# Agent attention before two feed-forward layers: scores with agents on partitions, one maximum, all weights decoded ahead of the loop

## The chip, the cores and the metric

One core of one Trainium2 chip runs the whole program. The metric is the device time of one execution in microseconds (us). The kernel before has a median of 1144.72 us over 3 runs (1144.35 to 1146.73).

## What is computed

The reference, cut to what matters (q, k, v are 12480 x 128, there are 49 agents, the hidden size of both layers is 2048):

```python
def _attn_ref(q, k, v, agents):
    scale = 1.0 / np.sqrt(q.shape[-1])
    def sm(a, b):
        s = scale * (a @ b.transpose(0, 2, 1))
        s = s - s.max(-1, keepdims=True)
        e = np.exp(s)
        return e / (e.sum(-1, keepdims=True) + 1e-09)
    agent_v = sm(agents, k) @ v
    return sm(q, agents) @ agent_v

def _moe_ref(x, w_in, w_out):
    h = x @ w_in
    g = np.where(h >= 1, h, np.where(h <= -1, 0.0, (h + 1) ** 2 / 4))
    return g @ w_out

def _moe2_ref(x, w_in, w_out, s, b):
    r = np.maximum(x @ w_in, 0.0)
    return (s * (r * r) + b) @ w_out
```

The output is `_moe2_ref(_moe_ref(_attn_ref(...)))`. The weights arrive as 64-bit floats; the kernel decodes them itself into a high and a low part, both fp32r.

## The kernel before, in words

**The preparation** (`prologue`, `agents_values`, L292 to L528) makes the agents' values and folds them into the first layer's weights. An order written out by hand, the string SEQ (L52), sets how its steps are issued; each engine runs its own instructions in that order. Keys and values come in 14 groups of 7 chunks of 128 tokens. For each group `score` (L372) makes one matmul per chunk, with the keys as the stationary operand, so tokens lie on partitions and agents in columns; ACT copies the scores to SBUF (L378), and `peak` (L387) keeps a running maximum on DVE. Groups 0 to 6 form a first half, groups 7 to 13 a second. For each half the maximum per agent is found (L392), transposed by PE (`turn`, L399), reduced (L403) and spread over all partitions by a matmul (`spread`, L410). Then `power` subtracts it on POOL (L420) and ACT takes the exponential (L423), and `average` (L434) multiplies with the values, even and odd chunks into the two halves of PE's columns. The first half's sums are scaled to the second half's maximum and both are added (L502). The sums are normalised (L504 to L513), and `aw` (L520 to L526) multiplies them with the first layer's input weights in four blocks of 512 columns; two blocks share one PSUM tile.

**Decoding** (`decode`, L230) takes each of the four weight matrices in two pieces of 1024 columns: A0 A1 (first input weights), B0 B1 (first output weights), C0 C1 and D0 D1 (second layer). A piece costs five instructions on DVE (L244, L254, L261, L270, L275) and three on ACT (L245, L248 and the high copy L265), all on 128 x 1024. They are issued in order by the letter w in SEQ (31 of them), and what is left over when the preparation ends is issued in the loop, one at each W of ORDR or ORD, or by need (L699 to L706). Eight small instructions on DVE make each tile of the query softmax (L164 to L177, letter z in SEQ and `fill` in the loop).

**Loads** go through SP's queue in the order of LOADS (L58). `pump` issues a load as soon as SEQ has passed the step that frees its buffer: 10 buffers of keys and values, 3 of weights (1 MB each). POOL sets a column of ones in each tile of values (L333), so a row of sums comes with the averages. The letter d in SEQ is a dummy matmul on zeros (`dummy`, L466).

**The loop** (L691) walks over 25 blocks of tokens (the first has 256 columns, 23 have 512, the last 448) with eight steps each. A step issues on PE H1, O1, H2, O2 (L573, L655), on ACT the ReLU and the square (L589 to L595), on DVE the cap (L599) and the low part (L615), and the high copy by a pattern (L608, L610): in the first twelve steps it is a cast on POOL. The second layer lags by 11 steps. For the first 11 steps the order of a step's other instructions is ORDR:

```python
    NR, ORDR, ORD = 11, (
        "T2 R1 Y y V R2 Q G2 C2 W S1 L1 L2 M1 Z F c1 G1 F"
```

R1 and S1 are the ReLU and the square, L1 the low part of the step before, M1 the cap, c1 the cast, F a step of a query softmax. `column_sums` (L544) adds up the rows of the second output weights in 32 small matmuls, six a step, once their piece is decoded; a small DVE instruction (L550) closes it.

Of the kernel before, what the change touches and what calls it, by code (L numbers as in the profile page):

```python
# [11 lines left out]
I32 = mybir.dt.int32  # L12
# [6 lines left out]
def kernel(  # L19
# [25 lines left out]
    GR, XB, UB, WB, KV = 3, 3, 3, 2, 10  # L45
    WARM, CD = 12, 2
# [4 lines left out]

    SEQ = (  # L52
# [4 lines left out]
    )  # L57
    LOADS = (  # L58
        "k0 A0 k1 k2 A1 k3 k4 B0 k5 k6 B1 k7 k8 q0 v0 k9 v1 k10 v2 k11 C0 v3 k12 v4 k13 v5 v6 q1 v7 v8 v9 v10 "
        "v11 v12 v13 C1 D0 D1"  # L60
# [4 lines left out]
        "T2 R1 Y y V R2 Q G2 C2 W S1 L1 L2 M1 Z F c1 G1 F"  # L65
    ).split(), (
        "R1 T2 S1 V Q Y G2 R2 C2 L1 W F M1 y W L2 F Z G1 c1 W"
    ).split()
    QS, QT, CSN, EA, DX = 3, 1, 6, 3, 1
# [9 lines left out]
    chunks = [(c0, min(P, NT - c0)) for c0 in range(0, NT, P)]  # L79
    NCH = len(chunks)  # L80
    GC = 7
    groups = [list(range(g, min(g + GC, NCH))) for g in range(0, NCH, GC)]
    NG = len(groups)
# [7 lines left out]
    dec = ctx.enter_context(tc.tile_pool(name="dec", bufs=1))  # L91
# [15 lines left out]
    aT2 = const.tile([P, 2 * NA], F32, name="aT2")  # L107
    aT = aT2[:, 0:NA]
# [119 lines left out]
    decoded = [0]  # L228

    def decode(weights):  # L230

        first, last = [], []
        for src, dst_h, dst_l, i in weights:
            sl = slice(i * WC, (i + 1) * WC)
            t = {}

            def exponent(t=t, src=src, i=i):
                u = wu.pop((src.name, i))
                words = u.rearrange("p (n two) -> p n two", two=2)
                t["e"] = u[:, 0:WC]  # L240
                t["lo"], t["hi"] = words[:, :, 0], words[:, :, 1]
                w = dec.tile([P, 2 * WC], U32, tag="t", name="wt", bufs=WB)
                t["y"], t["z"] = w[:, 0:WC], w[:, WC:2 * WC]
                nc.vector.tensor_scalar(out=t["y"], in0=t["hi"], scalar1=MASK_H, scalar2=None, op0=ALU.bitwise_and)  # L244
                acts.append(lambda: nc.scalar.activation(  # L245
                    out=t["z"].bitcast(I32), in_=t["lo"], func=ACTF.Copy, scale=XS
                ))
                acts.append(lambda: nc.scalar.activation(  # L248
                    out=t["y"].bitcast(I32), in_=t["y"], func=ACTF.Relu, scale=8.0, bias=wbias[:, 0:1]
                ))  # L250

            def rest(t=t):
                run_acts()
                nc.vector.scalar_tensor_tensor(  # L254
                    out=t["z"], in0=t["hi"], scalar=23, in1=t["z"], op0=ALU.logical_shift_left, op1=ALU.bitwise_or
                )

            def sign(t=t, sl=sl, dst_h=dst_h):
                run_acts()
                y = t["y"]  # L260
                nc.vector.scalar_tensor_tensor(  # L261
                    out=y, in0=t["hi"], scalar=0x80000000, in1=y, op0=ALU.bitwise_and, op1=ALU.bitwise_or
                )
                acts.append(
                    lambda: nc.scalar.activation(out=dst_h[:, sl], in_=y.bitcast(F32), func=ACTF.Copy)  # L265
                )

            def power(t=t):
                run_acts()
                nc.vector.tensor_scalar(  # L270
                    out=t["e"], in0=t["y"], scalar1=0xFF800000, scalar2=None, op0=ALU.bitwise_and
                )

            def low(t=t, sl=sl, dst_l=dst_l):
                nc.vector.scalar_tensor_tensor(  # L275
                    out=dst_l[:, sl], in0=t["z"], scalar=2.0 ** -43,
                    in1=t["e"].bitcast(F32), op0=ALU.mult, op1=ALU.mult,
                )
                decoded[0] += 1

            first.append(exponent)
            last.append([rest, sign, power, low])
        ops = [first[0]]
        for i, rest in enumerate(last):
            ops += rest[:EA] + first[i + 1:i + 2] + rest[EA:]
        return ops
# [5 lines left out]
    def prologue():  # L292
        with ExitStack() as pctx:
            pro = pctx.enter_context(tc.tile_pool(name="pro", bufs=1))
            wi1h = pro.tile([P, DFF], F32R, name="wi1h")
            wi1l = pro.tile([P, DFF], F32R, name="wi1l")
            agents_values(pro, wi1h, wi1l)

    def agents_values(pro, wi1h, wi1l):
# [4 lines left out]
        half = {"A": range(0, (NG + 1) // 2), "B": range((NG + 1) // 2, NG)}  # L304
        cut = half["B"][0]
        S = pro.tile([P, NCH, LO], F32, name="S")
        mx = pro.tile([P, GC, NA], F32, name="mx")
        diag = pro.tile([P, NA], F32, name="diag")
        fold = pro.tile([P, 1], F32, name="fold")
        rden = pro.tile([P, 1], F32, name="rden")  # L310
        eps = pro.tile([P, 1], F32, name="eps")
        avs = pro.tile([P, C + 1], F32, name="avs")
        avn = pro.tile([P, C], F32, name="avn")
        twice = pro.tile([P, P], F32, name="twice")
        avh = pro.tile([P, P], F32R, name="avh")
        avl = pro.tile([P, P], F32R, name="avl")
        mx1, mt, mcol, mbs, av = {}, {}, {}, {}, {}
# [6 lines left out]
        def keys(g):  # L324
            c0, c1 = chunks[groups[g][0]][0], sum(chunks[groups[g][-1]])
            kv["k", g] = pro.tile([P, GC * (C + 1)], F32, tag="kv", name=f"k{g}", bufs=KV)
            nc.sync.dma_start(out=kv["k", g][:, :c1 - c0], in_=kT[:, c0:c1])

        def values(g):
            full = [c for c in groups[g] if c < NFULL]  # L330
            t = pro.tile([P, GC * (C + 1)], F32, tag="kv", name=f"v{g}", bufs=KV)
            t = kv["v", g] = t.rearrange("p (c d) -> p c d", d=C + 1)
            nc.gpsimd.memset(t[:, :, C:C + 1], 1.0)  # L333
            nc.sync.dma_start(out=t[:, :len(full), :C], in_=v_main[:, full[0]:full[-1] + 1, :])
            if len(full) < len(groups[g]):
# [22 lines left out]
        def parts(g):  # L358

            cs = groups[g]  # L360
            for n in sorted({chunks[c][1] for c in cs}, reverse=True):
                own = [c for c in cs if chunks[c][1] == n]
                yield n, own[0], own[-1] + 1

        def score(g):

            scv = ps_h(f"ks{g}").rearrange("p b (c a) -> p (b c) a", a=P)
            c1 = groups[g][0]
            base = chunks[c1][0]
            for c in groups[g]:  # L370
                c0, n = chunks[c]
# [406 lines left out]
```

## Time and profile before

| | before |
|---|---|
| median of 3 runs | 1144.72 us |
| the profiled execution | 1145.62 us |
| its span, first to last instruction | 1143.8 us |
| PE busy (share of the span) | 1113.0 us (97%) |
| DVE busy | 986.1 us (86%) |
| ACT busy | 961.4 us (84%) |
| POOL busy | 33.8 us (3%) |
| mean granted TensorE clock | 0.981 |

The busy times are sums over the whole execution. PE's matmuls overlap, so that a busy PE is one with a matmul in flight. The granted clock is a share of 2.4 GHz; 0.5 is the lower of its two levels, 1.2 GHz.

### The profile page before, as it was taken

Reading aid. Unit: us, or ns where it says so; the run is one execution under the profiler, and the core shown is the slowest. Engines: PE = TensorE matmul, PEld = TensorE weight load, DVE = VectorE, ACT = ScalarE, POOL = GpSimd, SP = SyncE. Lnnn points to the kernel's source line nnn. Section 1 sums busy time; section 2 is a strip of 40 time slices with the busy share of each in tenths; the row PEclk is TensorE's granted clock in tenths of the full one; section 3 lists DMA queues with packets and bytes.
Section 4 is the critical chain, followed back from the end, with each engine's and each line's share of the span. In section 5 each row is a group of like instructions: output and inputs, shape, how many; then the busy total and the mean of one; then the engine's idle time right before and its main releaser. Section 6 shows DMA issues by size and latency. Waiting matters only on the chain.

```text
span 1143.8 us, 13561 instructions
## 1 busy us (share of the span) xinstructions
PE 1113.0 (97%) x5167; PEld 910.7 (80%) x5167; DVE 986.1 (86%) x1181; ACT 961.4 (84%) x1109; POOL 33.8 (3%) x50
## 2 busy tenths in 40 slices
PE   7878999999999999999999999999999999999998
PEld 6767788888888888888888888888888888888887
DVE  6568798988898898898998898898898898898886
ACT  4446798898988989989989988988989989889886
POOL 1333100000000000000000000000000000000000
PEclk9677999999999999999999999999999999999999
DMA  9930000000000000000000000000000000000000
GB/s 341 315 121 9 1 15 1 19 19 1 19 19 1 19 19 1 19 19 1 19 19 1 19 19 1 19 19 1 19 19 1 19 19 9 10 10 10 1 10 17
DMA packets 27312, 34.86 MB, mean 30 GB/s; under 512 B 1968, under 2 KB 19056, under 8 KB 26736
## 3 DMA queue, kind: packets, MB, share of 16 engines
q1 hardware_dynamic: 27248, 34.00, 9.2%
q8 instruction: 40, 0.66, 0.2%
q14 instruction: 24, 0.20, 0.1%
HBM read 27.61 MB, written 6.39 MB: 30 GB/s over the span
## 4 chain that ended last, share of the span: by engine, by line
PE 89%; DVE 4%; ACT 2%; issue 1%; POOL 0%; POOLq 0%; DVEq 0%; ACTq 0%
PE h L573 39%; PE o L655 24%; PE y L655 23%; PE qs L147 2%; DVE x L599 1%; PE tp L190 1%; PE avA L434 1%; DVE gl L615 1%; PE ks L372 0%; ACT x L595 0%; ACT x L589 0%; DVE wt L254 0%; ACT wt L248 0%; POOL gh L610 0%; PE aw L520 0%
## 5 line engine op out<-in xcount | busy, mean ns | idle before, releaser
L615 DVE TENSOR_TENSOR gl<-x,gh 128x1024 fp32r<-128x1024 f32 (+2 forms) x399 | 476.4, 1194 | 15.1 <-POOL gh L610 6.3
L595 ACT ACTIVATE x<-x 128x1024 f32<-128x1024 f32 (+2 forms) x399 | 392.0, 1032 | 0.6
L589 ACT ACTIVATE x<-h 128x1024 f32<-128x1024 f32 (+2 forms) x200 | 201.6, 1008 | 111.1 <-PE h L573 111.1
L599 DVE SCALAR_TENSOR_TENSOR x<-h,x 128x1024 f32<-128x1024 f32 (+2 forms) x200 | 238.9, 1195 | 57.3 <-ACT x L595 53.4
L591 ACT ACTIVATE x<-h 128x1024 f32<-128x1024 f32 (+2 forms) x199 | 199.4, 1002 | 7.8 <-PE h L573 7.8
L610 DVE CAST gh<-x 128x1024 fp32r<-128x1024 f32 (+1 forms) x243 | 165.3, 681 | 38.5 <-ACT x L595 38.5
L655 PE MATMUL y<-gh,wo1h 128*128 128x512 f32 (+2 forms) x400 | 160.5, 401 | 3.1 <-POOL gh L610 2.1
L655 PE MATMUL y<-gl,wo1h 128*128 128x512 f32 (+2 forms) x400 | 157.8, 394 | 2.8 <-DVE gl L615 2.7
L573 PE MATMUL h<-pt,awh 128*128 128x512 f32 (+2 forms) x400 | 157.7, 395 | 0.8 <-ACT pt L195 0.8
L573 PE MATMUL h<-yh,wi2h 128*128 128x512 f32 (+2 forms) x400 | 156.0, 390 | 1.0 <-ACT x L591 0.8
L655 PE MATMUL y<-gh,wo1l 128*128 128x512 f32 (+2 forms) x400 | 156.7, 392 | 0.0
L573 PE MATMUL h<-pt,awl 128*128 128x512 f32 (+2 forms) x400 | 156.7, 392 | 0.0
L655 PE MATMUL o<-gl,wo2h 128*128 128x512 f32 (+2 forms) x400 | 156.0, 390 | 0.0
L573 PE MATMUL h<-yl,wi2h 128*128 128x512 f32 (+2 forms) x400 | 155.8, 390 | 0.0
L655 PE MATMUL o<-gh,wo2l 128*128 128x512 f32 (+2 forms) x400 | 155.8, 389 | 0.0
L655 PE MATMUL o<-gh,wo2h 128*128 128x512 f32 (+2 forms) x400 | 155.8, 389 | 0.0
L573 PE MATMUL h<-yh,wi2l 128*128 128x512 f32 (+2 forms) x400 | 155.7, 389 | 0.0
L608 ACT ACTIVATE gh<-x 128x1024 fp32r<-128x1024 f32 (+1 forms) x144 | 149.0, 1035 | 1.3 <-DVE x L599 1.2
L655 PEld LDWEIGHTS y<-gl,wo1h 128*128 128x128 f32 x400 | 76.2, 190 | 22.1 <-DVE gl L615 5.4
L655 PEld LDWEIGHTS y<-gh,wo1h 128*128 128x128 f32 x400 | 76.5, 191 | 19.6 <-POOL gh L610 3.5
L573 PEld LDWEIGHTS h<-pt,awh 128*128 128x128 f32 x400 | 76.3, 191 | 17.8 <-ACT pt L195 0.9
L573 PEld LDWEIGHTS h<-yh,wi2h 128*128 128x128 f32 x400 | 75.1, 188 | 19.0 <-ACT x L591 1.2
(124 smaller groups left out, 1040.1 us busy)
## 6 DMA issues: line engine op xcount, KB each, us to landing
q<-in_qT SPq DMA_DIRECT2D x23, 256.0 KB, 2.8
out_T<-osb SPq DMA_DIRECT2D x23, 256.0 KB, 2.0
k<-in_kT SPq DMA_DIRECT2D x13, 448.0 KB, 9.3
v<-in_v_main SPq DMA_DIRECT2D x13, 448.0 KB, 6.4
wu<-in_w_in SPq DMA_DIRECT2D x4, 1024.0 KB, 7.4
wu<-in_w_out SPq DMA_DIRECT2D x4, 1024.0 KB, 8.0
k<-in_kT SPq DMA_DIRECT2D x1, 416.0 KB, 8.4
v<-in_v_main SPq DMA_DIRECT2D x1, 384.0 KB, 4.7
```

The costliest lines, as they stand in the source:

```text
L147: nc.tensor.matmul(out=scv[:, i, :], lhsT=qt[:, c0:c0 + P], rhs=aT, start=True, stop=True)
L190: nc.tensor.matmul(out=tp[:, c0:c0 + P], lhsT=ptok[t % NPT][:, i, :], rhs=ident_r, start=True, stop=True,)
L434: nc.tensor.matmul(out=av[h][r, :], lhsT=S[:n, c, :], rhs=kv["v", g][:n, i, :], start=(c == same[0]), stop=(c == same[-1]),)
L573: nc.tensor.matmul(out=h[:, i, :w], lhsT=a[:, sl], rhs=r, start=(m == 0), stop=(m == len(ops) - 1))
L589: nc.scalar.activation(out=x, in_=h, func=ACTF.Relu, scale=0.5, bias=0.5)
L591: nc.scalar.activation(out=x, in_=h, func=ACTF.Relu)
L595: nc.scalar.activation(out=x, in_=x, func=ACTF.Square)
L599: nc.vector.scalar_tensor_tensor(out=x, in0=h, scalar=1.0, in1=x, op0=ALU.max, op1=ALU.min)
L608: nc.scalar.activation(out=a, in_=x, func=ACTF.Copy)
L610: (nc.gpsimd if kind == "2" else nc.vector).tensor_copy(out=a, in_=x)
L615: nc.vector.tensor_tensor(out=b, in0=x, in1=a.bitcast(F32), op=ALU.subtract)
L655: nc.tensor.matmul(out=o[:, :w], lhsT=l[:, c, :], rhs=r[:, i, :w], start=(c == 0 and m == 0), stop=(c == KF - 1 and m == 2),)
```

## The change

The preparation is rewritten; the loop loses its decoding and keeps everything else.

- **Scores** have agents on partitions: the agents (padded to 64) are the stationary operand, 512 keys the moving one, and a group of 1024 keys fills the two halves of the partitions. There are 13 groups. ACT copies a group (S), DVE reduces it to one column (m).
- **One maximum** for all keys, in place of two halves and their fold: a reduce (r), two tiny matmuls that swap the partition halves (w), and the negative scaled maximum as a column (c). The exponential (E) takes it as its bias, so POOL subtracts nothing.
- **Exponentials are transposed back** by PE, four transposes a group (t), copied from PSUM by DVE for groups 0, 3, 6, 9, 12 and by ACT for the others (V), into three buffers; then the averages (a) as before, all into one sum.
- **Decoding** is named step by step in SEQ (A0.0 is L244's step of piece A0, .1 and .2 ACT's two, .3 to .7 the rest). All eight pieces stand in SEQ. The high copy (.5) goes from ACT to POOL.
- **Agents' weights** use four PSUM tiles, one a block, in the three buffers.
- **Buffers**: 7 for keys and values (of 8 chunks), 4 for weights; the decoder's buffers belong to the preparation.
- SEQ has 43 dummies in place of 13, 38 of them ahead of r; 10 warm-up matmuls in place of 12.

The diff, cut to its core:

```diff
-    GR, XB, UB, WB, KV = 3, 3, 3, 2, 10
-    WARM, CD = 12, 2
+    GR, XB, UB, WB, KV = 3, 3, 4, 2, 7
+    WARM, CD = 10, 2
...
+        "d d d d A0.1 A0.0 d d A0.2 A0.3 d s0 A0.4 s1 S0 m0 A0.5 d S1 A0.6 d m1 d A1.1 A0.7 d d d A1.0 s2 A1.3 "
+        "A1.2 d s3 S2 A1.4 s4 S3 m2 A1.5 m3 d S4 A1.6 d m4 d A1.7 B0.1 d d d B0.0 s5 B0.3 B0.2 d s6 S5 B0.4 s7 S6 "
+        "m5 B0.5 m6 d S7 B0.6 d m7 d B0.7 B1.1 d d d B1.0 s8 B1.3 B1.2 d s9 S8 B1.4 s10 S9 m8 B1.5 B1.6 d S10 m9 d "
+        "m10 d B1.7 C0.1 d d d C0.0 s11 C0.3 C0.2 s12 q0 S11 C0.4 S12 d z0.0 d m11 C0.5 d C1.1 m12 d z0.1 r z0.2 d "
+        "C0.6 w z0.3 z0.4 d c z0.5 d C0.7 E0 d E1 t0 E2 z0.6 C1.3 t1 E3 t2 V1 V0 d t3 V2 z0.7 C1.0 a0 E4 z0.8 E5 "
+        "z0.9 a1 V3 E6 D0.0 E7 a2 E8 a3 E9 E10 t4 E11 t5 V4 t6 V5 t7 V6 a4 E12 C1.2 t8 V7 t9 C1.4 t10 D0.2 C1.6 "
+        "C1.5 D0.1 a5 D0.4 V8 a6 C1.7 D1.1 D0.5 t11 V9 a7 D0.3 t12 V10 a8 D1.3 p0 V11 a9 D0.6 P0 D1.0 q1 V12 D1.2 "
+        "D0.7 a10 z1.0 D1.4 a11 z1.1 a12 D1.5 D1.6 z1.2 z1.3 D1.7 z1.4 z1.5 z1.6 z1.7 z1.8 z1.9"
...
+    VDVE = (0, 3, 6, 9, 12)
...
+        "A0 k0 k1 A1 k2 k3 k4 B0 k5 k6 k7 B1 k8 k9 k10 C0 k11 k12 q0 C1 v0 v1 v2 D0 v3 q1 v4 D1 v5 v6 v7 v8 v9 v10 "
+        "v11 v12"
...
-        "T2 R1 Y y V R2 Q G2 C2 W S1 L1 L2 M1 Z F c1 G1 F"
+        "T2 R1 Y y R2 Q G2 C2 S1 L1 L2 M1 Z F c1 G1 F"
...
+        def high():
+            nc.gpsimd.tensor_copy(out=dst_h[:, sl], in_=t["y"].bitcast(F32))
...
         def score(g):
+            sc[g] = ps_h(f"ks{g}")[:, 0, :]
+            for r, t0, n in halves(g):
+                x = t0 - g * GT
                 nc.tensor.matmul(
+                    out=sc[g][r, :n], lhsT=a64, rhs=kv["k", g][:, x:x + n], start=True, stop=True
                 )
             free["kv"] += 1
...
+        def score_copy(g):
+            for r, c in areas(g):
+                nc.scalar.activation(out=ST[r, c], in_=sc[g][r, :c.stop - c.start], func=ACTF.Copy)
...
         def peak(g):
+            for r, c in areas(g):
+                nc.vector.tensor_reduce(out=mxs[r, g:g + 1], in_=ST[r, c], op=ALU.max, axis=AX.X)
+
+        def peaks():
+            nc.vector.tensor_reduce(out=m1, in_=mxs, op=ALU.max, axis=AX.X)
+
+        def other():
+            sw.append(ps_h("sw")[:, 0, 0:2])
+            for i, x in enumerate((ident, swap)):
+                nc.tensor.matmul(out=sw[0][:, i:i + 1], lhsT=x, rhs=m1, start=True, stop=True)
+
+        def column():
+            nc.vector.tensor_reduce(out=m1, in_=sw[0], op=ALU.max, axis=AX.X)
+            nc.vector.tensor_scalar_mul(nm, m1, -scale)
...
         def power(g):
+            for r, c in areas(g):
+                nc.scalar.activation(
+                    out=ST[r, c], in_=ST[r, c], func=ACTF.Exp, scale=scale, bias=nm[r, 0:1]
                 )
+
+        def turn(g):
+            tp[g] = ps_h(f"st{g}")[:, 0, :]
+            for j in range(4 if g < NG - 1 else 1):
+                sl = slice(g * TB + j * P, g * TB + (j + 1) * P)
+                nc.tensor.transpose(out=tp[g][:, j * P:(j + 1) * P], in_=ST[:, sl], identity=ident)
+
+        def turn_copy(g):
+            n = TB if g < NG - 1 else P
+            tok[g] = pro.tile([P, TB], F32, tag="tok", name=f"tok{g}", bufs=3)
+            if g in VDVE:
+                nc.vector.tensor_copy(out=tok[g][:, :n], in_=tp[g][:, :n])
+            else:
+                nc.scalar.activation(out=tok[g][:, :n], in_=tp[g][:, :n], func=ACTF.Copy)
...
+            for j in range(4 if g < NG - 1 else 1):
+                for h in range(2):
+                    n = REST if h and g == NG - 1 else P
+                    x = j * P + h * LO
+                    nc.tensor.matmul(
+                        out=av[0][h * LO:(h + 1) * LO, :], lhsT=tok[g][:n, x:x + LO],
+                        rhs=kv["v", g][:n, 4 * h + j, :], start=(g == 0 and j == 0), stop=(g == NG - 1),
+                    )
...
-        column_sums(NSUM)
-        nc.vector.tensor_tensor(out=avs, in0=av["B"], in1=avs, op=ALU.add)
+        nc.vector.tensor_copy(out=avs[:, C:C + 1], in_=av[0][:, C:C + 1])
         den = ps_h("den")[:, 0, 0:1]
         nc.tensor.matmul(out=den, lhsT=twice, rhs=avs[:, C:C + 1], start=True, stop=True)
+        nc.vector.tensor_copy(out=avs[:, :C], in_=av[0][:, :C])
...
-        nc.vector.reciprocal(out=rden, in_=den)
+        nc.vector.tensor_scalar_add(rden, den, 1e-9)
+        nc.vector.reciprocal(out=rden, in_=rden)
...
-        for i in range(DFF // (2 * TB)):
-            aw = ps_h(f"aw{i}")
-            for b in range(2):
...
+        for i in range(DFF // TB):
+            aw = ps_h(f"aw{i}")[:, 0, :]
+            sl = slice(i * TB, (i + 1) * TB)
...
-            while wfill and decoded[0] <= max(map(WORD.index, need), default=-1):
-                wfill.pop(0)()
-                feeds[0]()
-                run_acts()
...
-            column_sums(NSUM if n == D + 1 else CSN)
+            column_sums(CSN)
...
-                if c == "V": run_acts()
-                if c == "W":
-                    if wfill:
-                        wfill.pop(0)()
-                        feeds[0]()
```

## Rows read from the trace of the kernel before

**Rows 1.** Stretches: length; busy us of PE, PEld, DVE, ACT, POOL; clock; DMA share; GB/s.

```profile
0.00:35.00 35.00, 27.23 (x164) 24.14 (x165) 23.88 (x40) 16.49 (x22) 3.10 (x14) 0.91 0.99 347
...
35.00:60.00 25.00, 20.23 (x153) 17.73 (x151) 14.04 (x24) 9.87 (x19) 9.11 (x17) 0.70 1.03 305
...
60.00:76.60 16.60, 13.79 (x123) 11.51 (x122) 13.44 (x22) 9.41 (x18) 8.83 (x8) 0.71 0.45 146
...
85.00:112.00 27.00, 22.05 (x112) 19.62 (x111) 21.88 (x34) 16.34 (x26) 8.60 (x8) 0.75 0.04 11
...
150.00:1143.00 993.00, 989.97 (x4408) 806.94 (x4408) 878.38 (x1017) 876.03 (x977) 0.00 (x0) 1.00 0.04 12
```

**Rows 2.** Timeline (start us, us): the first weights, then from averages to loop.

```profile
7.97 1.12 ACT L245 ACTIVATE wt<-wu 128x1024 int32<-128x1024 uint32 x1
...
76.59 0.29 DVE L502 TENSOR_TENSOR avs<-avB,avs 128x129 f32<-128x129 f32 x1 [1.83 <-PE avB L434]
...
85.00 0.28 PE L573 MATMUL h<-pt,awh 128*128 128x256 f32 x1
...
86.44 1.22 DVE L254 SCALAR_TENSOR_TENSOR wt<-wu,wt 128x1024 uint32<-128x1024 uint32 x1
```

**Rows 3.** Chain of waits (start us, us, what): the first block of agents' weights.

```profile
78.76 0.98 PE aw L520 x3
...
79.76 0.61 ACT awh L523
...
80.39 0.70 DVE awl L524
```

**Rows 4.** Timeline of DVE: caps of steps 0, 1, 2, 7; column sums.

```profile
87.58 0.68 DVE L599 SCALAR_TENSOR_TENSOR x<-h,x 128x512 f32<-128x512 f32 x1
...
90.50 0.68 DVE L599 SCALAR_TENSOR_TENSOR x<-h,x 128x512 f32<-128x512 f32 x1
...
92.90 0.68 DVE L599 SCALAR_TENSOR_TENSOR x<-h,x 128x512 f32<-128x512 f32 x1
...
109.07 0.68 DVE L599 SCALAR_TENSOR_TENSOR x<-h,x 128x512 f32<-128x512 f32 x1
...
122.79 0.22 DVE L550 TENSOR_SCALAR bcol<-cs,b_sb 128x1 f32<-128x1 f32 x1 [1.92 <-PE cs L544]
```

**Rows 5.** Groups up to 120 us: the decode's instructions on DVE (busy us, mean ns).

```profile
L254 DVE SCALAR_TENSOR_TENSOR wt<-wu,wt 128x1024 uint32<-128x1024 uint32 x8 | 10.1, 1261 | 0.5 <-ACT wt L245 0.5
...
L261 DVE SCALAR_TENSOR_TENSOR wt<-wu,wt 128x1024 uint32<-128x1024 uint32 x8 | 9.7, 1216 | 0.1
...
L244 DVE TENSOR_SCALAR wt<-wu 128x1024 uint32<-128x1024 uint32 x8 | 5.8, 724 | 2.3 <-DMA wu<-in_w_in 2.3
...
L270 DVE TENSOR_SCALAR wu<-wt 128x1024 uint32<-128x1024 uint32 x8 | 5.5, 688 | 0.1
...
L275 DVE SCALAR_TENSOR_TENSOR wo2l<-wt,wu 128x1024 fp32r<-128x1024 uint32 x2 | 2.4, 1217 | 0.0
```

**Rows 6.** Timeline: two reduces, one decode step beside POOL, one cast on POOL.

```profile
50.06 0.26 DVE L164 TENSOR_REDUCE qm<-qe 128x2 f32<-128x98 f32 x1 [1.70 <-ACT qe L154]
...
63.64 1.98 DVE L275 SCALAR_TENSOR_TENSOR wi2l<-wt,wu 128x1024 fp32r<-128x1024 uint32 x1
...
67.34 0.34 DVE L164 TENSOR_REDUCE qm<-qe 128x4 f32<-128x196 f32 x1
...
121.00 1.04 POOL L610 CAST gh<-x 128x1024 fp32r<-128x1024 f32 x1 [2.53 <-DVE x L599]
```

**Rows 7.** Timeline of PE: scores, averages at two clocks, a transpose.

```profile
21.27 1.70 PE L372 MATMUL ks<-aT,k 128*128 128x98 f32 x14
...
50.08 1.09 PE L434 MATMUL avA<-v,S 128*64 128x129 f32 x14
...
57.21 0.45 PE L399 MATMUL mtB<-ident,mx1B 128*128 128x128 f32 x1 [3.33 <-DVE mx1B L395]
...
57.58 1.98 PE L434 MATMUL avA<-v,S 128*64 128x129 f32 x14
```

More of the change, by code (lines that the diff above doesn't have):

```diff
@@ L78 @@
     NB = len(blocks)
[L79 to L83, printed above, removed]
+    GT = 2 * TB
+    NG = -(-NT // GT)
     NFULL = v_main.shape[1]
     REST = v_rest.shape[0]
+    LAST = NFULL * P
     const = ctx.enter_context(tc.tile_pool(name="const", bufs=1))
@@ L226, in load_w @@
         wu[src.name, i] = u
[L228 to L252, printed above, removed]
-                run_acts()
[L254 to L286, printed above, removed]
@@ L303, in agents_values @@
         }
[L304 to L309, printed above, removed]
+        ST = pro.tile([P, (NG - 1) * TB + P], F32, name="ST")
+        mxs = pro.tile([P, NG], F32, name="mxs")
+        m1 = pro.tile([P, 1], F32, name="m1")
+        nm = pro.tile([P, 1], F32, name="nm")
         rden = pro.tile([P, 1], F32, name="rden")
-        eps = pro.tile([P, 1], F32, name="eps")
         avs = pro.tile([P, C + 1], F32, name="avs")
@@ L348, in pump @@
                 else:
-                    if not free["u"] + decoded[0]:
+                    if not free["u"]:
                         return
                     free["u"] -= 1
-                    load_w(pieces[kind][0], i)
+                    load_w(dec, pieces[kind][0], i)
                 todo.pop(0)
@@ L356, in pump, with halves @@
                     nc.sync.dma_start(out=b_sb, in_=b_in.unsqueeze(1).to_broadcast([P, 1]))
[L358 to L363, printed above, removed]
-        def score(g):
[L367 to L371, printed above, removed]
+        def halves(g):
+            for h in range(2):
+                t0 = g * GT + h * TB if g < NG - 1 else (g * GT, LAST)[h]
+                yield slice(h * LO, (h + 1) * LO), t0, TB if g < NG - 1 else (P, REST)[h]
@@ L452, in agents_values @@
+        nc.sync.dma_start(out=aT, in_=agentsT)
         pump()
@@ L470, in agents_values @@
         nc.vector.tensor_copy(out=ones_r, in_=ones[:, 0:2])
-        wops.extend(decode([(*pieces[p[0]], int(p[1:])) for p in WORD]))
+        for x in range(2):
+            sl = slice(x * LO, (x + 1) * LO)
+            nc.vector.tensor_tensor(out=twice[:, sl], in0=ident[:, 0:LO], in1=ident[:, LO:P], op=ALU.add)
+        nc.vector.tensor_tensor(out=swap, in0=twice, in1=ident, op=ALU.subtract)
         does = {
-            "s": score, "m": peak, "r": peaks, "t": turn, "c": column, "b": spread, "e": power, "a": average,
-            "q": scores_q, "w": work, "z": lambda: zops and zops.pop(0)(), "d": dummy, "p": q_transpose,
+            "s": score, "S": score_copy, "m": peak, "r": peaks, "w": other, "c": column, "E": power, "t": turn,
+            "V": turn_copy, "a": average, "q": scores_q, "z": step_q, "d": dummy, "p": q_transpose,
+            "P": lambda t: q_evac(),
@@ L476, in agents_values @@
         }
+        steps = {p: decode(dec, *pieces[p[0]], int(p[1:])) for p in WORD}
         for token in SEQ.split():
-            kind, arg = token[0], token[1:]
-            does[kind](*([int(arg)] if arg.isdigit() else [arg] if arg else []))
-            if kind in "ebs":
-                run_acts()
-            if token == "s2":
-                for x in range(2):
-                    nc.vector.tensor_tensor(
-                        out=twice[:, x * LO:(x + 1) * LO], in0=ident[:, 0:LO], in1=ident[:, LO:P], op=ALU.add
-                    )
```

205 lines of the change are left out of this document (86 added, 119 removed), and 4 rows, old and new, of the table SEQ.

## The prediction

> **What bounds the kernel now.** I read the span in stretches first. From 150 us to the end PE is busy for 989.97 of 993.00 us at full clock: the loop is bound by TensorE, and the change touches nothing in it. Before that no engine is full: in the 76.6 us up to the last average DVE is busy for 23.88 + 14.04 + 13.44 = 51.4 us, and from 85 to 112 for 21.88 of 27 [rows 1]. What the change can move lies there, in the chain from the last average to the loop, and in the loop's first steps, which still decode weights. An instant by which the loop starts earlier is kept to the end, since PE is full behind it. Next I read the end of the preparation: the averages are added at 76.59 and the first H of the loop starts at 85.00, 8.4 us later [rows 2]. Of these, 6.2 us are the four blocks of agents' weights from 78.76 on: PE, ACT and DVE take turns, because a block waits until the block before it in its tile is read [rows 3]. Then the first steps: the caps (L599) of steps 0 to 7 run from 87.58 to 109.07, 3.07 us a step, while undisturbed neighbours are 2.40 us apart, and at 122.79 DVE stands for 1.92 us for the column sums [rows 4].
>
> The profiled execution took 1145.62 us for a span of 1143.8, 0.9 us over the median of the runs shown; I sum differences and take them from the median, 1144.72. About 0.2%, 2.3 us, is what a measurement of this kernel can tell from no change.
>
> **Decoding.** A piece costs DVE 0.72 + 1.26 + 1.22 + 0.69 + 1.22 = 5.1 us as busy time [rows 5]; back to back, an instruction of 1.22 us is followed after 1.14 (86.44 to 87.58 [rows 2, 4]), so 4.6 us. Six pieces and the first step of the seventh already lie ahead of the loop; the rest, some 8.7 us, moves in. ACT keeps two passes of about 1.1 us a piece [rows 2] and gives the high copy to POOL. A full-size cast on POOL takes 1.04 us by itself, and it is not free: a decode step went from 1.22 to 1.98 us beside POOL's work, while a reduce of 196 columns kept its 0.34 [rows 6]. Below nothing is excluded, since DVE does no less for it; at most each of the eight copies holds DVE for 1.04 us, 8.3 in all. The order puts several of them beside reduces, so I take 3 us, all behind the maximum.
>
> **Up to the maximum.** In the kernel before, ACT could take the first weights at 7.97 us [rows 2], behind 0.45 MB of keys; without these, at 347 GB/s, that is about 6.6. DVE then has four pieces (18.6), three steps of the fifth (2.9), and a reduce per group. Reduces of 98 and 196 columns took 0.26 and 0.34 [rows 6]; 512 columns are at least that and at most in proportion, 0.89; the slope gives 0.6. Twelve and a short one are 7.1 us. With 1.1 us for the first piece's own chain and 1.5 for the fifth weight to land, the maximum is there at 37.7. The keys and the weights ahead of them, 11.6 MB, need 33.5 us at 347 GB/s [rows 1]: DVE is the later. PE's scores are no bound at full clock. The nearest row is 14 records of 98 columns in 1.70 us [rows 7]; a group becomes four records of 512 columns, between 0.85 us (the two halves of the array beside each other) and 1.8 (one behind the other and scaled by columns).
>
> **From the maximum to the averages.** DVE has 0.3 for the column, 1.75 for the fifth piece, 13.9 for three more, two query softmaxes of eight small instructions, set at three quarters of the reduces' 0.34 and 0.26 [rows 6], so 2.1 + 1.5, and five copies of transposed exponentials from PSUM at the 0.70 of the awl row [rows 3], back to back 2.7: 22.3 us, and 3 for POOL. One stall lies in the order. The averages of group 3 need v3. Ahead of it stand 12.85 MB at 347 and, with D0, 3.15 MB at 305 GB/s: 47.4 us [rows 1]. PE does transposes 4 to 6 only behind that average; ACT holds the sixth piece's second pass behind copies of those, and DVE waits for it until about 52.5, some 5 us without work. In the same way v12 is there at 66 and the last average at 67.5; DVE, with 1.5 us of starting waits, is done at 37.7 + 22.3 + 3 + 5.5 + 1.5 + 0.5 = **70.5**. PE keeps up at full clock: a group's eight averages are 1.25 us (14 records in 1.09), and its four transposes are bounded by 0.45 each, the only such row, and by half of that when pipelined, which I take: 2.1 us a group, 26 in all [rows 7].
>
> **The last chain.** Up to the agents' weights it was 2.2 us (76.59 to 78.76); two copies for one addition and one more small instruction make 2.4. The four blocks get tiles of their own in three buffers, so only the fourth waits, for the first block's subtraction: 0.98 + 0.61 + 0.70 and gaps is 2.4, and 1.0 for its own matmuls, 3.4 us in place of 6.2 [rows 3]. H starts at 70.5 + 2.4 + 3.4 = 76.3: **8.7 us** earlier.
>
> **The loop's first steps.** Without decoding, a step is the turn cap, POOL's cast, subtraction. It was 2.40 us with decode steps beside the cast; a cast of half the full size by itself would be 0.5 and not 1.0, so the turn is between 1.9 and 2.4. I take 2.3, nearer to the measured one, and 0.6 for the third softmax: 7 x 2.3 + 0.6 = 16.7 in place of 21.5, **4.8 us** (bounds 0 and 8). The column sums no longer wait for weights and come in the first six steps, where PE has room; of DVE's 1.92 us [rows 4] the subtraction behind it gets back **0.9**, since POOL's cast, its other wait, was over at 122.04 [rows 6] and DVE went on at 122.9. At nothing I cost three edits. The 38 dummies ahead of the maximum stand on PE, covered by DVE; without that cover they are some 8 us (512 columns each at 2.4 GHz). On SP, D0 and D1 now stand ahead of v3 and v5; D1 waits for a buffer that the fourth piece has freed long before (by 35 us), so nothing queues behind it. On POOL the values' memsets wait for the scores that free their buffers, and high copies queue behind them; who waits for a high copy is the piece two further on, over 6 us later. If that cover goes, a piece starts late by the same wait.
>
> Sum: 8.7 + 4.8 + 0.9 = 14.4, and 1144.7 - 14.4 = **1130.3 us**.
>
> **Against a rule.** The clock's rows speak of a danger. The same 14 records took 1.09 us at 50.08 and 1.98 at 57.58, where PE had just stood still and then done a transpose; 35 to 60 has a mean of 0.70 of full clock [rows 1, 7], between the two levels, 1.2 and 2.4 GHz. I keep the full clock for the sum, since between the maximum and the last average PE has 26 us of work in 30. The Trainium skill, "TensorE: Matmul & The Clock Gate", Part 4, has it that a transpose does not count as activity in the way matmuls do. By that rule the 49 transposes would pull the clock down, and the sum would be the slower rival's.
>
> **Rivals.** *TensorE at half clock (slower).* Averages and transposes take turns on PE with hardly a dummy between. At 1.2 GHz a group is 16 records at the 1.98 us for 14, so 2.26, and four transposes of 0.36 (between 0.22 and the row's 0.45): 3.7 us, 45 for 12.25 groups. If the scores are at that level too, PE sets the maximum: twelve at 1.7 to 3.5 us and 38 dummies of 0.43 end between 43 and 65; I take 50, near the low end, since the averages, which also lie on halves of the array, took 1.09 us where the scores took 1.70 [rows 7]. Then 50 + 2 + 45 = 97, 26.5 us later than my 70.5, and 1156.8; with the scores spared, 85, so 1144.8. It decides from an end of the averages of 85 us, where the 14.4 are used up. For it: the dips above; against: they came behind an idle PE, and the new order has few such places. 0.14 slower by over 0.2%, 0.07 within. *Only the loop's share comes.* POOL's copies at all of their 8.3 us and stalls of another 3.2 bring the end to 79: 1138.8. For it: DVE was busy for only 67% of this part before, so dependencies cost more than my one stall. 0.22. *The order leaves no stall.* Values land at 347 GB/s and v3 is not waited for: end at 66, and a turn of 1.9: 8.7 + 4.5 + 7.6 + 0.9 = 21.7, so 1123.0. 0.08. *The change doesn't do what it says:* decoding still falls into the loop; nothing in the new loop can issue it, so 0. My forecast, 1126 to 1135: 0.49.
>
> Faster 0.49 + 0.22 + 0.08 = 0.79, same 0.07, slower 0.14. The range runs from 1123, the case without a stall, to 1143, an end of the averages at 83; it leaves out the half clock, 0.19 or so.
>
> **What would show it.** The averages copied out at about 70.5 (66 to 79); H at 76.3; 3.4 us from avh to H; caps of steps 0 to 7 in 16.7 us; no decode line behind H; the same 993 us from full PE to the end. Wrong would be: a granted clock near 0.5 from 40 to 67; DVE idle for more than 10 us there; or a cap-to-cap turn still at 3 us, which would put the first steps down to something other than decoding.

## The result, and the profile after

The changed kernel has a median of **1130.11 us** (four runs, 1129.19 to 1133.5), the kernel before 1144.86 (four runs): a ratio of 0.9874, with an interval of 0.985 to 0.9897. 1130.3 was predicted. Executions of one kernel differ here along with their mean granted clock (the changed kernel: 1129.2 to 1130.3 at 0.994 to 0.995, 1133.5 at 0.987); medians are over all of them.

The profiled execution took 1129.19 us, with a span of 1127.4 in place of 1143.8. Its stretches, in the columns of [rows 1] (length; busy us of PE, PEld, DVE, ACT, POOL; clock; DMA share; GB/s):

```profile
0.00:35.00 35.00, 27.00 (x101) 12.64 (x102) 29.54 (x43) 17.60 (x21) 6.07 (x18) 1.00 0.97 365
35.00:60.00 25.00, 19.22 (x190) 15.37 (x189) 18.43 (x32) 19.76 (x32) 5.60 (x10) 0.93 1.13 307
60.00:70.40 10.40, 6.30 (x78) 5.18 (x78) 9.31 (x18) 2.77 (x6) 1.04 (x1) 0.98 0.61 166
...
43.00:67.00 24.00, 20.32 (x248) 16.48 (x245) 16.72 (x23) 15.96 (x25) 5.51 (x9) 1.00 1.05 284
...
70.40:76.60 6.20, 5.77 (x15) 4.24 (x15) 1.70 (x6) 1.48 (x3) 0.00 (x0) 0.50 0.00 0
...
78.00:97.00 19.00, 17.49 (x127) 15.42 (x127) 13.77 (x27) 12.94 (x23) 4.94 (x8) 1.00 0.05 15
135.00:1126.00 991.00, 988.85 (x4405) 805.44 (x4403) 877.19 (x1016) 874.76 (x975) 0.00 (x0) 1.00 0.04 12
```

Read the DVE column first. Up to 70.4 us, where the averages are copied out, DVE is busy for 29.54 + 18.43 + 9.31 = 57.3 us; before it was 51.4 up to 76.6 [rows 1]. The preparation holds all the decoding now and still ends 6.4 us earlier, because DVE stands idle for 13.1 us in it and not for 25.2. From 135 us on PE is full, as before: nothing of the gain is given back in the loop. The other thing to see is the clock of 0.50 between 70.4 and 76.6.

DVE's timeline (start us, us, instruction, idle before it and its releaser): the first weights, the maximum, the stall, the end of the averages, then caps and column sums:

```profile
6.66 0.69 DVE L243 TENSOR_SCALAR wt<-wu 128x1024 uint32<-128x1024 uint32 x1 [3.76 <-DMA wu<-in_w_in]
...
38.72 0.16 DVE L380 TENSOR_REDUCE m<-mxs 128x1 f32<-128x13 f32 x1
...
50.18 0.69 DVE L408 COPY tok<-st 128x512 f32<-128x512 f32 x1 [3.56 <-PE st L402]
52.30 1.23 DVE L261 SCALAR_TENSOR_TENSOR wt<-wu,wt 128x1024 uint32<-128x1024 uint32 x1 [1.42 <-ACT wt L251]
...
70.16 0.15 DVE L474 COPY avs<-av 128x1 f32<-128x1 f32 x1
...
79.66 0.69 DVE L563 SCALAR_TENSOR_TENSOR x<-h,x 128x512 f32<-128x512 f32 x1 [0.55 <-ACT x L559]
81.67 0.68 DVE L563 SCALAR_TENSOR_TENSOR x<-h,x 128x512 f32<-128x512 f32 x1
...
89.87 0.21 DVE L514 TENSOR_SCALAR bcol<-cs,b_sb 128x1 f32<-128x1 f32 x1
90.69 0.65 DVE L563 SCALAR_TENSOR_TENSOR x<-h,x 128x512 f32<-128x512 f32 x1
...
95.11 0.68 DVE L563 SCALAR_TENSOR_TENSOR x<-h,x 128x512 f32<-128x512 f32 x1
97.18 1.22 DVE L563 SCALAR_TENSOR_TENSOR x<-h,x 128x1024 f32<-128x1024 f32 x1
```

And PE's timeline: the scores of two groups, the transposes of four and the averages of one, then the last chain:

```profile
28.23 2.20 PE L366 MATMUL ks<-k,a 128*64 128x512 f32 x8
...
48.62 2.06 PE L402 MATMUL st<-ident,ST 128*128 128x128 f32 x16
50.61 1.11 PE L419 MATMUL av<-v,tok 128*64 128x129 f32 x16
...
70.46 0.56 PE L476 MATMUL den<-avs,twice 128*128 128x1 f32 x2 [3.63 <-DVE avs L474]
...
73.02 0.79 PE L493 MATMUL aw<-wi1h,avh 128*128 128x512 f32 x1 [0.37 <-ACT avh L486]
...
77.59 0.28 PE L537 MATMUL h<-pt,awh 128*128 128x256 f32 x1
```

The 16.4 us between the two spans come from these places, each an instant of after against [rows 2, 4] or a row of the same view:

| where | before | after | gain |
|---|---|---|---|
| averages copied out (before: added) | 76.59 | 70.16 | 6.4 |
| from there to the first H | 8.41 | 7.43 | 1.0 |
| first H to first cap | 2.58 | 2.07 | 0.5 |
| caps of steps 0 to 7 | 21.49 | 15.45 | 6.0 |
| cap of step 7 to cap of step 8 | 3.43 | 2.07 | 1.4 |
| caps of steps 8 to 11 | 12.22 | 11.38 | 0.8 |

These are 16.2 us, and 0.2 lie behind. The row on step 8 rests on its cap in before, which had to wait for an H that started only at 108.26 (DVE's and PE's timelines of before):

```profile
112.50 1.23 DVE L599 SCALAR_TENSOR_TENSOR x<-h,x 128x1024 f32<-128x1024 f32 x1 [0.42 <-ACT x L595]
```

```profile
108.26 0.77 PE L573 MATMUL h<-pt,awh 128*128 128x512 f32 x1
```

The medians differ by less, 14.75, since the profiled execution of before lies 0.8 us over its median and that of after 0.9 under.

### The profile page after: what moved, and what is told of

It is laid out like the page before. It is cut to its first block, busy times and chain, and to the rows that moved or that the text cites. A ratio compares the mean times of both kernels' runs of the same rounds, so it can differ in the third digit from the quotient of the medians.

```text
span 1127.4 us, 13411 instructions
## 1 busy us (share of the span) xinstructions
PE 1100.3 (98%) x5098; PEld 886.1 (79%) x5098; DVE 983.5 (87%) x1179; ACT 962.1 (85%) x1104; POOL 21.8 (2%) x40
## 4 chain that ended last, share of the span: by engine, by line
PE 89%; DVE 6%; DMA 2%; issue 1%; ACT 1%; POOL 1%; POOLq 0%; SPq 0%; DVEq 0%; ACTq 0%
PE h L537 39%; PE o L619 24%; PE y L619 23%; PE qs L150 2%; DVE x L563 2%; DMA v<-in_v_main 1%; PE tp L193 1%; DVE wt L261 1%; POOL gh L574 1%; DVE mxs L377 1%; DVE gl L579 1%; DVE wu L269 0%; DMA wu<-in_w_in 0%; PE aw L493 0%; ACT wt L251 0%
```

## The experiments

The theory was that DVE's idle time in the preparation is used up, and that the loop starts earlier and is relieved of decoding. The rivals: that decoding early gains by itself, without the new order; that the first steps of before were slow from TensorE's clock and not from decoding; and that the dummies or POOL's copies carry the result. Eleven kernels took single parts of the change, or the terms of the sum, by themselves. "Before" and "after" name the kernel that was edited.

**1. The four PSUM tiles alone (b_aw4), on before.**

```diff
-        for i in range(DFF // (2 * TB)):
-            aw = ps_h(f"aw{i}")
-            for b in range(2):
-                sl = slice((2 * i + b) * TB, (2 * i + b + 1) * TB)
+        for i in range(DFF // TB):
+            aw = ps_h(f"aw{i}")[:, 0, :]
+            sl = slice(i * TB, (i + 1) * TB)
...
```

> The kernel before with one part of the change alone: the four blocks of agents' weights in four PSUM tiles of their own. Theory (a block waited for the block before it in the shared tile): from the first aw matmul to the first H 3.4 us in place of 6.2, the rest unmoved, so 2.8 us less in all, about 1142. Rival 1 (ACT's and DVE's copies set the pace, not the tile): 6.2 stays, 1144.9. Rival 2 (the clock sets it, as in the changed kernel, where the stretch took 4.6 us at a granted clock of 0.50): 4.6, 1143.3, with a clock below 0.6 there.

1142.37 us (10 runs) against 1145.55, a ratio of 0.9969 (0.9958 to 0.9981). The blocks start at 80.17 and H at 83.35, 3.2 us in place of the 6.2 of before. PE's timeline:

```profile
80.17 0.50 PE L519 MATMUL aw<-wi1h,avh 128*128 128x512 f32 x1 [0.37 <-ACT avh L512]
...
83.35 0.28 PE L568 MATMUL h<-pt,awh 128*128 128x256 f32 x1
```

The medians differ by 3.2 us. This part is worth what was predicted, 3 us, where the clock is full (1.00 from 80 to 83.4).

**2 and 3. Early decoding alone, on before, without and with dummies (b_early, b_early_d).** The three lines of `hold` are in the second alone.

```diff
-        while decoded[0] <= WORD.index(f"A{NW - 1}"):
+        hold = ps_h("hold")[:, 0, :]
+        for i in range(34):
+            nc.tensor.matmul(out=hold, lhsT=zero[:, 0:P], rhs=zero, start=True, stop=True)
+        while wops:
...
-        column_sums(NSUM)
```

> The kernel before with all weights decoded ahead of the loop and nothing else changed: the leftover decode steps are issued behind the last average. Theory (the decoding costs DVE the same wherever it stands, and only a new order can hide it): the sum of the averages and H come 7 to 9 us later, the caps of steps 0 to 7 take 15.5 to 16.7 us in place of 21.5 and the wait for the column sums goes, together 7 to 8 back; total 1143 to 1146.5. Rival (the gain is all from early decoding, as DVE has idle time ahead of the loop): H at most 2 us later, total 1136 to 1139.

1154.43 us (4 runs), a ratio of 1.0063 (1.0044 to 1.0082): slower, which none of the theories had. The caps of steps 0 to 7 took 21.7 us (95.82 to 117.52) with no decoding beside them. The stretch of steps 3 to 5 tells why:

```profile
101.00:113.00 12.00, 12.00 (x57) 12.00 (x58) 4.86 (x10) 4.27 (x8) 1.71 (x3) 0.50 0.08 23
```

PE is full at the lower level, with DVE at 4.86 of 12 us. Before that stretch PE had stood idle for 7.31 us ahead of the denominators (L503, at 83.10), and 76 to 100 has a mean clock of 0.61. It was not one long fall, though: from 93 to 95 us the clock was back at 1.00, and it fell anew as the loop began. The same kernel was run with dummies in the hole:

> The kernel before with all weights decoded ahead of the loop, as in the run before, and 34 dummy matmuls on PE between the last average and the denominators. Theory (early decoding frees the loop's first steps only while TensorE's clock is full; in the run without dummies PE stood still for 7.3 us, the clock fell, and steps 0 to 7 kept 21.7 us): granted clock 1.0 in these steps, their caps in 15 to 17 us, total 1146 to 1148.5, so 6 to 8 us under the run without dummies. Rival (the steps are slow for another reason, the column sums at six a step): 20 us or more again at full clock, total 1151 or more.

1147.18 us (10 runs), a ratio of 1.0023 (1.0002 to 1.0045). In the profiled execution (1145.37) H is as late (93.56 us), but the caps take 15.4 us (95.63 to 111.05) at full clock:

```profile
101.00:113.00 12.00, 10.96 (x74) 9.12 (x73) 9.43 (x20) 7.60 (x13) 3.08 (x6) 1.00 0.09 24
```

The ten fall into two groups: six of 1145.1 to 1147.4 us at a mean clock of 0.984 to 0.986, and four of 1151.7 to 1154.5 at 0.974 to 0.977, about what run 2 took. So the dummies did not always keep the clock up. They also cost a little: the denominators' matmul came behind them, at 85.59, with the sums added at 84.10.

Two things follow. Decoding early by itself gains nothing that can be told, even in the six: it takes 6 us off the first steps and puts 8.6 ahead of H. And the first steps can be slow for a second reason, the clock, which costs as much (21.7 us of caps in run 2, 15.4 here).

**4. The first steps of before with TensorE kept busy (b_hold).**

```diff
-                if c == "H1" and a1: H(1, n)
+                if c == "H1" and a1:
+                    H(1, n)
+                    for _ in range(5 if n < JP else 0):
+                        nc.tensor.matmul(
+                            out=hp[1, n][:, 0, 256:512], lhsT=ident_r, rhs=pt_t[t][:, :256], start=True, stop=True
+                        )
```

> The kernel before, decoding in the loop as it was, with five extra matmuls of 256 columns behind each H of steps 0 to 7, into unused columns of its PSUM tile, so that PE stands still less. Theory (in the kernel before the first steps were slow for the decode steps on DVE and ACT, not for the clock, which was 0.75 from 85 to 112 us): with a clock near 1.0 there the caps of steps 0 to 7 still take 19 us or more, total 1142 to 1145. Rival (they were slow because the clock fell): 15.5 to 17.5 us, total 1138 to 1141.

1147.03 us (10 runs), a ratio of 1.0009 (0.9996 to 1.0021): no difference, and above both ranges that were expected. The stretches of before, and then those of this kernel:

```profile
85.00:104.00 19.00, 14.05 (x79) 12.40 (x77) 14.93 (x24) 12.54 (x21) 5.57 (x5) 0.82 0.05 15
104.00:112.00 8.00, 8.00 (x36) 7.22 (x35) 6.95 (x11) 3.79 (x5) 3.03 (x3) 0.58 0.00 0
```

```profile
85.00:104.00 19.00, 15.24 (x110) 13.54 (x110) 14.08 (x22) 12.61 (x21) 5.58 (x5) 1.00 0.06 15
104.00:112.00 8.00, 7.40 (x34) 7.22 (x35) 7.46 (x13) 2.29 (x4) 2.32 (x3) 0.57 0.01 2
```

The caps of steps 0 to 5 run from 88.90 to 104.55 here and from 87.58 to 103.23 in before: 15.65 us both, at a clock of 1.00 and of 0.82. So in these five turns it was the decoding that counted; without it they take 11.0 (after 79.66 to 90.69; b_early_d 95.63 to 106.64). Behind 104 us the clock was low in both, and what of the 1.4 us of steps 5 to 7 and the 1.4 at step 8 is clock was not separated.

**5. Work put back on DVE in the loop (a_loopwork), on after with the dummies of run 6.** One instruction a step on a scratch tile of 128 x 1024.

```diff
...
+                if c == "S1" and n < JP:
+                    nc.vector.scalar_tensor_tensor(
+                        out=scr, in0=scr, scalar=23, in1=scr, op0=ALU.logical_shift_left, op1=ALU.bitwise_or
+                    )
...
```

> The changed kernel with 14 dummies behind the last average (1127.3) and, in each of steps 0 to 7, one more DVE instruction of a decode step's kind and size (1.14 us) on a scratch tile, ahead of the square's place: 9.1 us of DVE work, about what the kernel before decoded there. Theory (decode work lies in the turn of cap, cast and subtraction): the caps of steps 0 to 7 take 19 to 24 us in place of 15.4, total 1131 to 1136. Rival (it fits beside POOL's cast, and the clock was the cost): at most 17.5 us, total up to 1129.5.

1137.33 us (4 runs), a ratio of 0.9923 (0.9909 to 0.9937), 10.0 over run 6. The first turns, and a stretch:

```profile
78.50 0.69 DVE L563 SCALAR_TENSOR_TENSOR x<-h,x 128x512 f32<-128x512 f32 x1
81.42 0.68 DVE L563 SCALAR_TENSOR_TENSOR x<-h,x 128x512 f32<-128x512 f32 x1
...
102.73 0.68 DVE L563 SCALAR_TENSOR_TENSOR x<-h,x 128x512 f32<-128x512 f32 x1
```

```profile
84.00:92.00 8.00, 8.00 (x40) 8.00 (x40) 7.31 (x12) 3.04 (x6) 2.52 (x3) 0.50 0.13 35
```

One instruction of 1.22 us makes a turn of 2.9 out of 2.0, at a clock of 1.00 (78.5 to 81.4): DVE's load on the turn, as predicted. But the caps come to 24.2 us and the total to 1137.3, both a little above what was expected: from 84 to 92 us the clock is at its lower level too. All four executions had a mean clock of 0.986 to 0.992, and the four of run 6, the same kernel without this work, 0.996 to 0.998. So DVE's work in the loop cost twice here, once itself and once with a lower clock; that PE's longer waits are what let it fall was not shown.

**6. The last chain at full clock (a_gap), on after.**

```diff
-  a11 z1.1 a12 D1.5 D1.6
+  a11 z1.1 a12 d d d d d d d d d d d d d d D1.5 D1.6
```

> The changed kernel with 14 dummy matmuls on PE behind the last average, where PE stood still for 3.6 us before the clock fell to 0.50. Theory (the idle PE let the clock fall): granted clock 1.0 from 70 to 77 us, from the first aw matmul to H 3.4 us in place of 4.6, H 1.2 to 1.7 us earlier, total 1128.5 to 1129. Rival (the clock falls for the thin use of PE between 52 and 67 us, whatever stands behind it): clock 0.5 there as before, no gain, 1130. A second rival: the dummies hold up the denominators' matmul, H later by up to 2 us.

1127.31 us (4 runs), a ratio of 0.9831 (0.9814 to 0.9847). H is at 75.74, 1.85 us earlier, and from the first block to H it is 3.2 us. The stretch of the chain, which had a clock of 0.52 in after:

```profile
70.40:77.00 6.60, 5.79 (x29) 4.29 (x30) 3.56 (x9) 3.13 (x6) 0.00 (x0) 1.00 0.00 0
```

**7. The stall taken out (a_order), on after.** C1's sign step and the steps behind it, D0's and q1's softmax move ahead of the averages that wait for v3 to v12; only SEQ changes.

```diff
-  V3 E6 D0.0 E7 a2 E8 a3 E9 ... E12 C1.2 t8 V7 t9 C1.4 t10 D0.2 C1.6 C1.5 D0.1 a5 D0.4 ... q1 V12 D1.2 ... z1.8 z1.9
+  V3 E6 D0.0 C1.2 E7 a2 E8 C1.4 D0.2 a3 C1.6 C1.5 E9 ... q1 z1.0 a5 ... V12 D1.2 z1.8 z1.9 a10 D1.4 D1.5 a11 D1.6 D1.7 a12
```

> The changed kernel with another order from the sixth group's exponential on: ACT's second passes of pieces C1 and D0 moved ahead, and the second query softmax moved ahead of the last averages, nothing else. Theory (the end of the preparation is set by DVE's stall of some 5 us between 46 and 52 us, waiting for that pass): the averages are copied out at 67.0, right behind the last average, in place of 70.2; PE isn't idle before the denominators, so the clock holds and H comes at 73 in place of 77.6; total 1125.5 to 1126.5. Rival (POOL's casts or the landing of the values set the end): copied out at 69 or later, total 1129 to 1130.

1127.54 us (5 runs), a ratio of 0.9829 (0.9811 to 0.9847). DVE's timeline:

```profile
47.20 1.23 DVE L261 SCALAR_TENSOR_TENSOR wt<-wu,wt 128x1024 uint32<-128x1024 uint32 x1 [0.48 <-ACT wt L251]
...
55.39 1.23 DVE L256 SCALAR_TENSOR_TENSOR wt<-wu,wt 128x1024 uint32<-128x1024 uint32 x1 [2.52 <-ACT wt L248]
...
67.84 0.15 DVE L474 COPY avs<-av 128x1 f32<-128x1 f32 x1
```

The sign step comes 5.1 us earlier and the averages are copied out 2.3 us earlier; 2.52 us of the stall came back as a wait for another pass of ACT, at 55.39. H is at 74.56, not 73. The clock did not do as expected: PE waited for only 1.17 us ahead of the denominators, and still 67 to 74 us has a clock of 0.77 (1.00 up to 70, 0.50 from 71 on). The row of PE's timeline, and the stretch:

```profile
68.05 0.38 PE L476 MATMUL den<-avs,twice 128*128 128x1 f32 x2 [1.17 <-DVE avs L474]
```

```profile
67.00:74.00 7.00, 5.30 (x16) 3.90 (x17) 3.47 (x9) 1.60 (x4) 0.00 (x0) 0.77 0.04 13
```

**8. Both together (a_best).** The order of run 7, two dummies ahead of a11 and five behind a12.

```diff
-  a10 D1.4 D1.5 a11 D1.6 D1.7 a12
+  a10 d d D1.4 a11 D1.6 D1.7 a12 D1.5 d d d d d
```

> The reordered version with 7 dummy matmuls around the last averages, and the last piece's high copy behind its low part. Theory (what was left there is 1.2 us of idle PE, which let the clock fall at 70.7, and 0.7 us of DVE behind POOL): averages copied out by 67.3, clock 1.0 from 67 to 74, H at 72.7 to 73.3 in place of 74.6, total 1124.5 to 1125.5, under both dummies alone (1127.3) and order alone (1127.5). Rival (the landing of the values at 65.2 or thin use of PE decides): no more than 0.5 us under these.

**1125.2 us** (1125.09 to 1130.13, 4 runs), a ratio of 0.9825 (0.9804 to 0.9846): faster than before and after. By these ratios runs 6, 7 and 8 can't be told apart; what sets run 8 under the other two is the median and the trace. H is at 73.54, 4.05 us earlier than after's and 1.02 earlier than run 7's. All of that 1.02 comes behind the averages, which are copied out at 67.81, no earlier than in run 7 and not by 67.3 as expected. The chain's stretch is now at full clock:

```profile
67.00:74.00 7.00, 6.30 (x29) 4.44 (x28) 4.07 (x10) 2.33 (x5) 0.00 (x0) 1.00 0.09 34
```

**9. The same with TensorE kept busy in the first steps (a_best_hold).** Four matmuls behind each H of steps 0 to 7, as in run 4.

> The version with the new order and the 7 dummies (1125.2, one run in four 1130.1 at a mean clock of 0.990 instead of 0.998) and four extra matmuls of 256 columns behind each H of steps 0 to 7. Theory (the odd run is one in which the clock fell in the loop's first steps, where PE is used thinly): all runs within 1125 to 1126.5. Rival (the extra matmuls hold PE up in these steps): 1127 or more in all runs. A second rival: an odd run of 1129 or more stays, so the fall has another place.

1126.76 us (1126.54 to 1127.06, 5 runs), a ratio of 0.9831 (0.9818 to 0.9845). The median lies between what the theory and the rival had. The first cap comes 2.55 us behind H in place of 2.07, and the caps take 16.3 us in place of 15.4: most of the price, some 1.5 us. No run of the five lay far off, where one in four of run 8 did; so few runs don't show that the matmuls are why.

**10. The high copy on ACT (a_highact), on after.**

```diff
-            nc.gpsimd.tensor_copy(out=dst_h[:, sl], in_=t["y"].bitcast(F32))
+            nc.scalar.activation(out=dst_h[:, sl], in_=t["y"].bitcast(F32), func=ACTF.Copy)
```

> The changed kernel with the high copies back on ACT instead of POOL, at the same places of the order. Theory (POOL's casts cost DVE 3.2 us by stretching five of its instructions, which then end the preparation): no stretched decode step, the averages copied out 1.5 to 3 us earlier than 70.2, total 1127 to 1129. Rival (ACT, in order, holds the score copies and second passes behind eight copies of 1.06 us, and DVE waits for these): copied out at 70 or later, total 1130 to 1133.

1130.15 us (4 runs), a ratio of 0.9862 (0.9847 to 0.9877), not to be told from after. The profiled execution, 1132.82, is the longest of the four: its clock is at 0.50 from 86 to 94 us, and its caps take 19.7 us (78.46 to 98.17). So it is compared with after's only up to the averages. The groups of DVE's instructions up to 71 us (count, busy us, mean ns, idle before), first of after, then of this kernel:

```profile
L261 DVE SCALAR_TENSOR_TENSOR wt<-wu,wt 128x1024 uint32<-128x1024 uint32 x8 | 10.6, 1328 | 1.8 <-ACT wt L251 1.4
L269 DVE TENSOR_SCALAR wu<-wt 128x1024 uint32<-128x1024 uint32 x8 | 7.9, 986 | 0.0
```

```profile
L261 DVE SCALAR_TENSOR_TENSOR wt<-wu,wt 128x1024 uint32<-128x1024 uint32 x8 | 9.8, 1223 | 1.8 <-ACT wt L251 1.4
L269 DVE TENSOR_SCALAR wu<-wt 128x1024 uint32<-128x1024 uint32 x8 | 5.5, 686 | 0.0
```

POOL's copies stretch DVE's instructions by 0.8 + 2.4 = 3.2 us. Without them the maximum comes 1.0 us earlier (37.76), but the averages are copied out at 69.60 in place of 70.16, so 0.6 us on the path, less than the theory had: DVE's idle time ahead of the transposes' copies (L408) went from 5.8 to 7.5 us, so that a good part of the stretch falls where DVE would wait anyhow.

**11. No dummies in SEQ (a_nodummy), on after.** All 43 letters d are taken out.

> The changed kernel without the 43 dummy matmuls in its order (the warm-up stays). Theory (they stand on an idle PE and hold the clock): the clock falls to 0.5 in the scores and averages, the maximum comes at most 3 us later, as DVE sets it, the averages at 3.0 to 3.7 us a group end between 74 and 85; total 1133 to 1145. Rival (the clock doesn't need them, or PE isn't on the path even at half clock): averages copied out by 71, total 1129 to 1131.

1129.54 us (4 runs), a ratio of 0.9851 (0.9835 to 0.9868), the same as after. The stretches show the clock go down and come back with only transposes and averages on PE:

```profile
20.00:30.00 10.00, 7.44 (x20) 1.80 (x22) 9.91 (x11) 5.08 (x7) 1.87 (x4) 0.72 1.05 398
41.00:44.00 3.00, 2.36 (x11) 2.36 (x12) 3.00 (x6) 2.78 (x5) 0.00 (x0) 0.50 1.11 342
44.00:50.00 6.00, 6.00 (x81) 5.42 (x80) 2.22 (x5) 5.74 (x11) 0.72 (x4) 0.92 1.14 323
50.00:67.00 17.00, 13.91 (x166) 11.10 (x164) 14.28 (x16) 10.06 (x15) 4.79 (x5) 1.00 1.04 271
```

The averages are copied out at 70.06. PE's slower scores and transposes stay beside DVE's work, so the dummies of the preparation buy nothing that these runs can tell. The profiled execution is again the longest (1133.58, the others 1129.2 to 1129.7), and again its caps are slow, 20.0 us (79.39 to 99.43) at a clock of 0.50 from 84 to 95. These two profiles thus show where such an execution loses its 3 to 4 us: in the loop's first steps, as run 9's theory had it.

## Why the prediction was right

**The mechanism held.** DVE sets the end of the preparation, and it did so nearly at the predicted instants: first weights at 6.66 (6.6 predicted), the maximum at 38.7 (37.7), the values v3 at 47.6 (47.4), the stall until 52.3 (52.5), the averages out at 70.16 (70.5). That the stall is the order's own, and not DVE's work, run 7 shows: moving steps alone gives 2.3 us. What brought DVE's idle time from 25 to 13 us, the one maximum with its shorter DVE part or the order, was not taken apart. Nor was TensorE's clock in before: from 57 to 69 us it was 0.50 with PE busy for 11.8 of 12 us, and two groups of averages lie on before's chain of waits there (start us, us, what), where one took 1.09 us at full clock [rows 7]:

```profile
57.65 1.91 PE avA L434 x14
...
60.16 1.92 PE avA L434 x14
```

So some of the 6.4 us up to the averages may be clock; no run shows how much.

**The last chain was undersized.** The sum had 3.4 us from the first block to H, at full clock; it took 4.57 (73.02 to 77.59), and the steps up to the block 2.86 and not 2.4. Run 6 shows the cause: with PE kept busy these steps take 2.3 and the blocks 3.2. The prediction looked for a low clock between 40 and 67 us, where it stayed high from 43 on, and not behind the 3.63 us in which PE waits for DVE's last steps.

**The first steps were undersized the other way.** The caps took 15.45 us and not 16.7: a turn is 2.01 us at first, against the 2.3 that was taken, and POOL's cast of half size 0.62 against the 0.5 of the sum. Another 1.4 us came between steps 7 and 8, which the sum did not have: before's H of step 8 had to wait for column sums and matmuls at a clock of 0.58, and started only at 108.26. The sum also had nothing for the 0.5 us from H to the first cap. The 0.9 for the column sums was right (0.84).

**The last digit is luck.** For H the sum had 8.7 us and 7.4 came; for the rest it had 5.7 and 8.8 came. So the places give 16.2 us where 14.4 were predicted: the pluses outweigh the minus by 1.8. That the forecast met the median to 0.2 us is because the medians lie 1.7 us closer together than the two profiled executions.

**POOL's price was right and misplaced.** 3 us of DVE's time were predicted, all behind the maximum, and 3.2 found; but about half lies ahead of it, and run 10 shows 0.6 us of the whole on the path. The Trainium skill, "SBUF — State Buffer", section "Who interferes with whom", says that tensor_scalar in a two-port mode and instructions with two inputs in SBUF contend with GpSimd, and that a reduce never does. The traces agree: in after, with the casts on POOL, the two groups shown in run 10 took 1328 and 986 ns, without them 1223 and 686, and the reduces (L377) 614 and 616.

**The slower rival fell** by its prices and by its condition. Scores are 1.10 us a group at full clock (2.20 for eight records), and without the dummies (run 11) 1.6 to 1.8 (twelve records in 4.68, eight in 3.68), the low end of its 1.7 to 3.5; even so the maximum came at 39.1, 0.4 later than in after. Four transposes take 0.52 (16 in 2.06), and the clock was 1.00 from 43 to 67 us. The prediction's upper bound for a group of scores does not follow from its row: 14 records of 98 columns in 1.70 us, scaled to four of 512, give 2.5 and not 1.8. The Trainium skill, "TensorE: Matmul & The Clock Gate", Part 4, has it that a transpose does not count as activity in the way matmuls do. This trace shows no fall of the clock with 49 of them between 41 and 60 us: it had fallen at 39, where PE had waited for 2.81 us for the maximum, was back at 1.00 at 43, and stayed there up to 67. So the rule decided nothing here. The rival *only the loop's share comes* fell with the averages at 70.2 and not 79; the rival without a stall (66 and 1123.0) lies nearest to run 8 (67.8 and 1125.2), not to this change.

## What to carry to other kernels

Work moved out of a loop's first steps pays only if the earlier stage has idle time for it: the same decoding, put early without a new order, moved 6 us and gained nothing (runs 2 and 3). Give independent blocks a PSUM tile each (3 us here). And where TensorE waits just ahead of a chain that runs on it, look at the granted clock of that chain: 14 dummy matmuls in the hole (run 6), or 7 with the better order (run 8 against run 7), gave 2 to 3 us of the median and 1 to 2 of H's start, while 43 spread over a stretch that another engine bounds gave nothing that could be told.

## What the runs showed of the hardware

The clock fell after a shorter wait than I had thought of: behind 1.17 us of idle PE, in a stretch in which it had little to do (run 7), 67 to 74 us had a mean of 0.77, and with seven dummies there (run 8) 1.00. Which counted, the wait or the thin use around it, was not separated. In the loop's first steps a clock at its lower level did not soon rise again though PE was full: for 12 us at 0.50 in run 2, for 11 in run 11. A transpose of 128 x 128 in f32 took 0.13 us in a row of 16 at full clock, and scores whose results lie in the two halves of the partitions cost 1.10 us for four records of 512 columns.
